# Where a fused attention and MLP kernel loads q, k and v: two quads at the head of each MLP stage, and an output ring of four

## The chip, the cores and the metric

The kernel runs on one core of a Trainium2 chip. The metric is the device time of one launch in microseconds (us); lower is better.

## The reference

Forgetting attention (causal attention whose scores get the sum of log forget gates between key and query), followed by an MLP with the tanh form of GELU:

```python
def _attn_ref(q, k, v, f):                    # each [8, 8, 576, 64]; f is [8, 8, 576]
    scores = scale * np.matmul(q, k.transpose(0, 1, 3, 2))
    cum = np.cumsum(np.log(np.clip(f, 0.0001, 1.0)), axis=-1)
    decay = cum[:, :, :, None] - cum[:, :, None, :]
    scores = np.where(causal, -1000000000.0, scores + decay)
    attn = softmax(scores)                    # written out with max, exp and sum
    return np.matmul(attn, v)

def _moe_ref(x, w_in, w_out):                 # x [4608, 512], w_in [512, 2048], w_out [2048, 512]
    h = x @ w_in
    return gelu_tanh(h) @ w_out

x = attn_out.transpose(0, 2, 1, 3).reshape(4608, 512)
out = _moe_ref(x, w_in, w_out)                # [4608, 512] float32
```

## The kernel before, in words

**Work.** The 64 heads (8 batches of 8) are taken in 16 *quads* of four heads; quad i belongs to batch i // 2. The 4608 rows of the MLP are taken in nine *chunks* of 512, numbered 0 to 8. q and k of a quad are loaded by GpSimd's DMA queue (`load_one`, line 192), which turns them from float32 to bfloat16 on the way, into `q_c` and `k_c`; v of a batch is loaded in five pieces of 128 rows (`load_v`, line 169) into `v_nat`, mostly on SP's queue. All three have two buffers: quad i uses buffer i % 2, batch b buffer b % 2. VectorE transposes q and k (line 198); the scores are matmuls (line 261), their exponentials ScalarE's (line 269), the causal mask is cut by GpSimd (line 275) or multiplied in by VectorE (line 304), `vw` is v times a weight (line 215), and two kinds of products with the exponentials (line 329) give denominators and attention output, which VectorE writes into `xT` (line 360). The first MLP product (lines 374, 422 and 464) goes through GELU on ScalarE into `gT`; the second (line 510; line 580 for chunk 0) goes through VectorE's additions (line 535) into a buffer of the ring `ostage` and is stored by SP (line 523).

**Order.** Everything is issued in an order written out by hand, each engine working through its own instructions in that order. `SETUP` and `FRONT` hold the start: quads 0 to 6 and the chunks 0 and 1. `TABLES[c]` holds chunk c, for c from 2 to 8. A word is an operation with its arguments:

- `LK.i`, `LQ.i`: load k or q of quad i (GpSimd's queue). `TK.i`, `TQ.i`: transpose it (VectorE). A load waits until the transpose that last read its buffer is done.
- `LV` (in a table, chunk c): load v of batch c + 2 (SP). `LV.b.h`: half h (four heads) of batch b on SP. `LX.b.h`: the same on GpSimd's queue. `@` names a load that must be done first.
- `S.i.r`, `M.i.r`, `m.i.r`: scores, mask on GpSimd, mask on VectorE, of round r. `D.i`: denominators. `V.i.x`: attention output. `VW.i`, `vw.i`: `vw` on GpSimd or VectorE.
- `I`, `P`, `R`: parts of a chunk's first MLP product. `G`, `U`, `K`, `T`: sums of blocks on VectorE, for a scheme that multiplies 2 by 2 blocks with seven products.
- `F.n`, `f.n`: the next n pieces of the chunk's second product. `O.512`: what is left of the second product of the chunk before.
- `Y`, `X`: the tables for GELU or the exponential are loaded.

In a table, `q3` stands for quad 2c + 3, `q4` for 2c + 4 and so on. What stands up to `X` is called the chunk's **MLP stage** here (O, P, R, G); what comes behind it is its **attention stage**, where scores and products of two quads lie between pieces of the chunk's second product. So chunk 3 loads quad 11 (`q5`) in its MLP stage and quad 12 (`q6`) in its attention stage, chunk 4 quads 13 and 14, chunk 5 quad 15; chunk 2 loads quads 9 and 10 in its MLP stage, behind the transposes of quads 7 and 8, whose loads stand at the end of `FRONT`. `q6` in chunk 5 and beyond names quads that there are not, and nothing is issued.

**What runs ahead.** A load stands in GpSimd's instructions among masks and `vw`; GpSimd gets to it when what stands ahead of it is done, which can be before TensorE has reached that place of the text.

The kernel text, with the lines of the profile:

Of the kernel before, what the change touches and what calls it, by code (L numbers as in the profile page):

```python
# [8 lines left out]
FP32 = mybir.dt.float32  # L9
# [7 lines left out]
def kernel(  # L17
# [12 lines left out]
    B, H, S, D = q.shape  # L30
    BH = B * H
# [40 lines left out]

    FRONT = """
        TQ.0 B.2.256 TK.1 SB TR LP.2@LQ.0 B.2.128 CW S.0.0 B.5.384 B.1.256 Z TQ.1 vw.0.0 S.0.2 WI.0 LQ.2 M.0.0 B.3.384 H.1.0.1 LP.3 B.1.256 vw.1.0
        WI.1@LU.4 W H.1.1.1 WI.3 B.2.256 WI.2 H.1.0.0 M.1.0.1 D.0.0 M.1.0.0 H.0.1.1 V.0.0.0 H.0.1.0 B.2.256 M.0.1 H.1.1.0 V.0.1.0 D.1.0 H.0.3.0 B.2.128
        V.1.0.0 LX.1.1 H.0.3.1 V.1.1.0 m.0.3.2 H.1.3.0 m.0.3.4 B.1.256 VW.1.1 H.1.3.1 B.4.128 vw.0.1 D.0.1 M.1.3 S.1.2 M.1.1 LK.2 V.0.1.1 V.0.0.1 WO.0
        J.0.1 D.1.1 J.0.0 WO.1@LV.1.1 V.1.1.1 V.1.0.1 J.0.3 WO.2@WI.1 VW.3 J.1.0 WO.3 LK.3 LQ.3 J.1.1 TQ.2 J.1.3 LQ.4 LX.1.0@WO.2 TK.2 J.0.2 J.1.2 X
        LK.4 F.0.6 TK.3 B.3.256 S.2.0 LK.5 F.0.9 S.2.2 F.0.10 S.2.1 TQ.3 TQ.4 F.0.10 LV.2.0@LK.5 m.2.1 vw.2 TK.4 S.3.0 f.0.1 M.2.2 CL.2 LQ.5 M.2.0 D.2
        f.0.6 S.3.1 m.3.0 F.0.6 V.2.0 S.3.2 TK.5 LK.6 M.3.2 f.0.7 V.2.1 CL.3 S.4.1 m.3.1 LQ.6 F.0.6 TQ.5 H.4.2.1 D.3 H.4.0.1 LQ.7 VW.4 H.4.0.0 V.3.1
        v.3.0 f.0.3 H.4.2.0 CL.4 I.1.0 m.4.1 U.0 LV.2.1@LQ.5 I.1.4 TQ.6 m.4.2.3 I.1.1 I.1.5 U.1 LV.3.0@LQ.7 m.4.2.2 TK.6 G.0 M.4.0 I.1.2 I.1.3 U.3  # L80
        I.1.6 I.1.7 G.1.1.2 U.2 X F.1.16 S.5.0 f.1.26 S.5.1 D.4 M.5.0 f.1.16 S.5.2 V.4.0 m.5.2.3 f.1.10 VW.5 V.4.1 CL.5 m.5.2.2 LQ.8 S.6.0 f.1.10 M.5.1
        D.5 f.1.7 S.6.1 V.5.1 f.1.12 V.5.0 vw.6 S.6.2 m.6.1 M.6.2.2 m.6.0 m.6.2.3 LK.7 LK.8 CL.6 LX.3.1@LK.6
    """

    HOMES = {1: 0, 3: 1}
# [5 lines left out]
    """  # L91
    TABLES[3] = """
        Y O.512 P.0.1 R.1 P.4.1 R.1 R.1 TK.q3 TQ.q3 LK.q5 LQ.q5 M.q2.2 LV P.2 G.0 P.3 P.6 P.7 G.1.1.2 X F.10 S.q3.0 D.q2 M.q3.0 f.22 S.q3.1 V.q2.0
        K.3.3 TK.q4 TQ.q4 M.q3.1 VW.q3 f.18 S.q3.2 V.q2.1 M.q3.2 TK.q5 LK.q6 LQ.q6 CL.q3 f.16 S.q4.0 VW.q4 D.q3 M.q4.0 f.18 S.q4.1 TQ.q5 V.q3.0 M.q4.1
        f.13 V.q3.1 T f.3 CL.q4 S.q4.2
    """
    TABLES[4] = """
        Y O.512 P.0.1 R.1 P.4.1 R.1 R.1 LK.q5 LQ.q5 M.q2.2 LV R.3 P.2.1 R.3 G.0.1.2 P.6 R.3 G.0.3.4 G.1.1.2 X F.10 S.q3.0 D.q2 M.q3.0 f.22 S.q3.1
        V.q2.0 TK.q4 TQ.q4 M.q3.1 VW.q3 f.18 S.q3.2 V.q2.1 M.q3.2 TK.q5 LK.q6 LQ.q6 CL.q3 f.16 S.q4.0 VW.q4 D.q3 M.q4.0 f.18 S.q4.1 TQ.q5 V.q3.0 M.q4.1
        f.13 V.q3.1 T f.3 CL.q4 S.q4.2  # L100
    """
    TABLES[5] = """
        Y O.512 P.0.1 R.1 P.4.1 R.1 R.1 LK.q5 LQ.q5 M.q2.2 LV R.3 P.2.1 R.3 G.0.1.2 P.6 R.3 G.0.3.4 G.1.1.2 X F.10 S.q3.0 D.q2 M.q3.0 f.22 S.q3.1
        V.q2.0 TK.q4 TQ.q4 M.q3.1 VW.q3 f.18 S.q3.2 V.q2.1 M.q3.2 TK.q5 LK.q6 LQ.q6 CL.q3 f.16 S.q4.0 VW.q4 D.q3 M.q4.0 f.18 S.q4.1 TQ.q5 V.q3.0 M.q4.1
        f.13 V.q3.1 T f.3 CL.q4 S.q4.2
    """
    TABLES[6] = """
        Y O.512 P.0.1 R.1 P.4.1 R.1 R.1 LK.q5 LQ.q5 M.q2.2 LV R.3 P.2.1 R.3 G.0.1.2 P.6 R.3 G.0.3.4 G.1.1.2 X F.10 S.q3.0 D.q2 M.q3.0 f.22 S.q3.1
# [7 lines left out]
    """  # L116

    singles = ctx.enter_context(tc.tile_pool(name="singles", bufs=1))
    ostage_pool = ctx.enter_context(tc.tile_pool(name="ostage", bufs=3))
    snap_pool = ctx.enter_context(tc.tile_pool(name="snap", bufs=4))  # L120
    den_pool = ctx.enter_context(tc.tile_pool(name="den", bufs=1))
    rb_pool = ctx.enter_context(tc.tile_pool(name="rb", bufs=2))
# [4 lines left out]
    def many(n, shape, dtype, name):  # L127
        return [singles.tile(shape, dtype, name=f"{name}{i}") for i in range(n)]
# [11 lines left out]
    vw = many(2, [128, NT + 1, 4, D], BF16, "vw")  # L140
# [4 lines left out]
    g1, g2, g4 = many(3, [128, HF, HC], BF16, "gsum")  # L145
    u1, u2, u4 = many(3, [128, HF, HD], BF16, "usum")
    w_in_sb = singles.tile([128, N_DT, D_FF], BF16, name="w_in_sb")
    w_out_sb = singles.tile([128, N_FT, D_MODEL], BF16, name="w_out_sb")
    f_sb = singles.tile([BH, S], FP32, name="f_sb")
    logfT = singles.tile([128, NT * BH], FP32, name="logfT")  # L150
    before = singles.tile([128, (NT - 1) * BH], FP32, name="before")
    wT = singles.tile([128, NQ, NT, 4], FP32, name="wT")
# [635 lines left out]
```

## Time and profile before

| | us |
|---|---|
| median of 3 runs | 331.43 |
| lowest and highest of them | 329.97, 331.58 |
| the profiled execution, its own time | 330.9 |
| its span, from the first to the last instruction | 329.2 |
| TensorE busy (matmuls) | 314.4 |
| VectorE, ScalarE, GpSimd busy | 241.3, 203.0, 111.6 |
| mean granted TensorE clock | 0.999 of full speed |

| stage (start to end in the span, us) | MLP | attention |
|---|---|---|
| chunk 2 | 102.57 to 116.39 | 116.39 to 138.30 |
| chunk 3 | 138.30 to 151.72 | 151.72 to 174.36 |
| chunk 4 | 174.36 to 187.53 | 187.53 to 208.94 |
| chunk 5 | 208.94 to 222.12 | 222.12 to 242.62 |

A stage starts here with its first matmul of the first or of the second product on TensorE. "Busy" of TensorE holds matmuls whose ends are modelled. In the profile's lists, a row of waits names an engine's instruction and what ended its idle time; "issue" is idle time that ended with nothing the profile shows. Of the DMA queues, q0 carries GpSimd's loads, q1 SP's loads and stores, and q8 the packets of kind "instruction". A share of the DMA engines is the time that packets took, over the time of 16 engines; it can come out over 100% where packets overlap.

### The profile page before, as it was taken

To read this page: it belongs to the slowest core of one execution; us is meant where nothing else is said; L and a number is where in the kernel's file an instruction comes from. 1 tells how busy PE (TensorE), PEld (TensorE's weight loads), DVE (VectorE), ACT (ScalarE), POOL (GpSimd) and SP (SyncE) were. 2 spreads that over 40 slices of the span, in tenths; PEclk is the share of its full clock that TensorE was granted. 3 is DMA by queue.
4 is the path that set the end of the run, shared out by engine and by line. 5 is a ranking of instruction groups with operands and counts; after the bars stand their busy time and mean duration, and the time that the engine had idled before them with its cause. 6 is when DMAs were issued, how large, how long until landed. Compare 5 with 4: busy or idle time off the path is not lost.

```text
span 329.2 us, 12196 instructions
## 1 busy us (share of the span) xinstructions
PE 314.4 (96%) x5479; PEld 214.8 (65%) x5499; DVE 241.3 (73%) x381; ACT 203.0 (62%) x245; POOL 111.6 (34%) x155
## 2 busy tenths in 40 slices
PE   3999999999999999999979999999999999999995
PEld 1357844544766467766766677667776787687684
DVE  4676139894867866878967899679977957785772
ACT  4685677775767576577647785668666951721630
POOL 8986563510414418202761038201820150000000
PEclk9999999999999999999999999999999999999999
DMA  7999999771124990184178415941020002012003
GB/s 119 210 215 214 171 230 206 149 167 31 36 40 94 234 208 31 66 177 75 36 149 172 68 37 106 193 92 36 8 95 0 26 14 98 0 35 96 3 32 98
DMA packets 44325, 33.45 MB, mean 102 GB/s; under 512 B 27488, under 2 KB 37856, under 8 KB 44272
## 3 DMA queue, kind: packets, MB, share of 16 engines
q0 software_dynamic: 8848, 16.58, 28.7%
q1 hardware_dynamic: 35280, 16.01, 18.6%
q8 instruction: 43, 0.70, 0.9%
q14 instruction: 10, 0.08, 0.1%
q10 hardware_dynamic: 144, 0.07, 0.1%
HBM read 36.85 MB, written 9.44 MB: 141 GB/s over the span
## 4 chain that ended last, share of the span: by engine, by line
PE 93%; POOL 2%; issue 2%; DVE 1%; DMA 1%; ACT 0%; POOLq 0%; DVEq 0%; ACTq 0%
PE ps_w L510 29%; PE ps_h L374 22%; PE ps_s L261 10%; PE po L329 10%; PE ps_cd L422 6%; PE ps_ab L422 5%; PE ps_h L464 4%; PE pso L580 4%; PE po_m L315 1%; PE idle_ps L240 1%; POOL v_nat L169 1%; DMA out_dram<-o_st 1%; PE ps_o L329 0%; DVE pt L304 0%; PE cum_ps L640 0%
## 5 line engine op out<-in xcount | busy, mean ns | idle before, releaser
L269 ACT ACTIVATE pt<-ps_s 128x1024 bf16<-128x1024 f32 (+2 forms) x100 | 93.7, 988 | 40.9 <-PE ps_s L261 36.4
L275 POOL TENSOR_SCALAR_AFFINE_SELECT pt<-pt 128x512 bf16<-128x512 bf16 (+3 forms) x65 | 39.2, 612 | 126.1 <-ACT pt L269 125.1
L374 PE MATMUL ps_h<-xT,w_in_sb 128*128 128x512 bf16 x320 | 75.7, 379 | 0.8
L381 ACT ACTIVATE gT<-ps_h 128x1024 bf16<-128x1024 f32 x42 | 42.9, 1022 | 41.1 <-PE ps_h L374 40.6
L374 PEld LDWEIGHTS <-w_in_sb 128*128 128x128 bf16 x336 | 32.8, 98 | 34.6 <-issue 0.4
L510 PEld LDWEIGHTS <-gT 128*32 128x32 bf16 (+1 forms) x1247 | 51.0, 97 | 6.7 <-issue 2.7
L510 PE MATMUL ps_w<-w_out_sb,gT 128*32 128x256 bf16 (+1 forms) x1050 | 47.2, 273 | 0.0
L510 PEld LDWEIGHTS <-gsum 128*32 128x32 bf16 (+1 forms) x1256 | 39.4, 97 | 1.4
L261 PE MATMUL ps_s<-qT,kT 32*128 32x64 bf16 (+5 forms) x896 | 36.7, 264 | 0.5 <-issue 0.4
L198 DVE STREAM_TRANSPOSE kT<-k_c 128x576 f32<-128x576 f32 x16 | 19.9, 1247 | 17.5 <-DMA k_c<-in_k_dram 17.5
L510 PE MATMUL ps_w<-usum,gsum 128*32 128x256 bf16 (+1 forms) x832 | 30.7, 273 | 0.0
L215 POOL TENSOR_TENSOR vw<-v_nat,wT 128x1280 bf16<-128x1280 f32 (+1 forms) x13 | 30.4, 2337 | 0.1
L535 DVE TENSOR_TENSOR o_st<-ps_w,snap 128x512 f32<-128x512 f32 x31 | 21.3, 690 | 10.7 <-PE ps_w L510 9.3
L261 PEld LDWEIGHTS <-kT 32*128 32x128 bf16 x896 | 16.7, 93 | 17.7 <-issue 12.9
L360 DVE TENSOR_TENSOR xT<-po,rb 128x576 bf16<-128x576 f32 x26 | 19.5, 752 | 9.5 <-PE po L329 9.0
L329 PE MATMUL po<-pt,vw 128*32 128x64 bf16 (+4 forms) x624 | 23.2, 278 | 1.7 <-issue 1.7
L329 PEld LDWEIGHTS <-vw 128*32 128x32 bf16 x672 | 14.5, 96 | 12.5 <-issue 6.0
L198 DVE STREAM_TRANSPOSE qT<-q_c 128x576 f32<-128x576 f32 x16 | 19.9, 1245 | 1.3 <-PE ps_s L261 0.7
L422 PEld LDWEIGHTS <-w_in_sb 128*128 128x128 bf16 x176 | 17.2, 98 | 5.1 <-issue 0.8
L431 ACT ACTIVATE gT<-snap 128x512 bf16<-128x512 f32 x33 | 18.9, 623 | 0.7
L510 PE MATMUL ps_w<-usum,gT 128*128 128x256 bf16 (+1 forms) x197 | 17.2, 273 | 0.7 <-issue 0.7
L169 POOL DMA_DIRECT2D v_nat<-in_v_dram x20 | 15.3, 776 | 4.7 <-DMA w_out_sb<-in_moe_w_out_dram 4.7
(100 smaller groups left out, 419.4 us busy)
## 6 DMA issues: line engine op xcount, KB each, us to landing
out_dram<-o_st SPq DMA_DIRECT2D x35, 256.0 KB, 2.6
k_c<-in_k_dram POOLq DMA_DIRECT2D x16, 288.0 KB, 5.4
q_c<-in_q_dram POOLq DMA_DIRECT2D x16, 288.0 KB, 6.0
v_nat<-in_v_dram SPq DMA_DIRECT2D x16, 256.0 KB, 5.1
w_in_sb<-in_moe_w_in_dram POOLq DMA_DIRECT2D x4, 512.0 KB, 10.1
w_out_sb<-in_moe_w_out_dram POOLq DMA_DIRECT2D x4, 512.0 KB, 8.4
v_nat<-in_v_dram SPq DMA_DIRECT2D x16, 128.0 KB, 3.3
v_nat<-in_v_dram POOLq DMA_DIRECT2D x13, 128.0 KB, 7.0
```

The lines of the kernel that those rows point to most:

```text
L198: nc.vector.transpose(out=dst.rearrange("p s c -> p (s c)").bitcast(FP32) .rearrange("p (t a) -> p a t", a=S // 32), in_=src.rearrange("p ...
L215: eng.tensor_mul(vw[i % 2][:, t0:t1], vb[:, t0:t1, h0:h0 + 4, :], wT[:, i, t0:t1, :].unsqueeze(3).to_broadcast([128, t1 - t0, 4, D]))
L261: nc.tensor.matmul(tiles[h // 2][:, h % 2, c0:c0 + nq], key_columns(i, key, h, c), qq[32 * h:32 * h + 32, q0:q0 + nq, c], start=(c == 0 an ...
L269: nc.scalar.activation(p[:, 2 * g:2 * g + 2, off:off + n], t[:, :, 0:n], AF.Exp, scale=scale)
L275: nc.gpsimd.affine_select(out=x, in_=x, compare_op=ALU.is_ge, fill=0.0, base=0, pattern=pattern, channel_multiplier=-1)
L329: nc.tensor.matmul(po[r0:r0 + w.shape[-1], 448 + q0:448 + q0 + nq], w, p[:, h, col:col + nq], start=(key in (0, "low")), stop=(key in ("lo ...
L360: nc.vector.tensor_mul(xT[:, 2 * u + x, S * b + s0:S * b + s1], po, rbs[i, part])
L374: nc.tensor.matmul(ph[:, j, :], w_in_sb[:, dt, 128 * ft:128 * ft + 128], xT[:, dt, CH * c:CH * (c + 1)], start=(dt == 0), stop=(dt == N_DT ...
L381: nc.scalar.activation(gT[:, 2 * pr:2 * pr + 2, :], ph, AF.Gelu_apprx_tanh)
L422: nc.tensor.matmul(ps[:, j], w[:, dt, 128 * j:128 * j + 128], x[:, dt], start=(first and j == 0 and dt == 0), stop=(dt == 1), skip_group_c ...
L510: nc.tensor.matmul(ps[c0:c0 + width, n, cols[0]:cols[1]], x[:, j, 128 * n + c0:128 * n + c0 + width], w[:, j, cols[0]:cols[1]], start=(fir ...
L535: nc.vector.tensor_add(st, ps, kept[name])
```

## The change

- `LK.q6 LQ.q6` leaves the attention stages of chunks 3, 4 and 5 (in chunk 5 it issued nothing). The MLP stages of chunks 4 and 5 get `LK.q4 LQ.q4` at their head, ahead of `LK.q5 LQ.q5`. Quads 12 and 14 are thereby loaded a stage later: together with 13 and 15.
- In `FRONT`, `LK.7 LQ.8 LK.8` move to chunk 1's MLP stage, behind `M.4.0`: `LQ.8` out of chunk 1's attention stage, the other two from the end.
- The second half of batch 3's v moves from the end of `FRONT` (`LX.3.1@LK.6`, on GpSimd's queue) to behind `LV.3.0`, as `LV.3.1` on SP's queue.
- The ring `ostage` has four buffers, not three. The 2 KB a partition that this takes come from `f_sb`, which has no tile of its own any more and lies in `g2`, a tile that is first written in chunk 1.

TensorE's and ScalarE's instructions stay the same, in the same order; so do VectorE's. Five DMA issues go from GpSimd to SP (`LV.3.1`). `TABLES[5]` has the same edit as `TABLES[4]`, and is left out of the diff below.

```diff
     FRONT = """
...
-        v.3.0 f.0.3 H.4.2.0 CL.4 I.1.0 m.4.1 U.0 LV.2.1@LQ.5 I.1.4 TQ.6 m.4.2.3 I.1.1 I.1.5 U.1 LV.3.0@LQ.7 m.4.2.2 TK.6 G.0 M.4.0 I.1.2 I.1.3 U.3
-        I.1.6 I.1.7 G.1.1.2 U.2 X F.1.16 S.5.0 f.1.26 S.5.1 D.4 M.5.0 f.1.16 S.5.2 V.4.0 m.5.2.3 f.1.10 VW.5 V.4.1 CL.5 m.5.2.2 LQ.8 S.6.0 f.1.10 M.5.1
-        D.5 f.1.7 S.6.1 V.5.1 f.1.12 V.5.0 vw.6 S.6.2 m.6.1 M.6.2.2 m.6.0 m.6.2.3 LK.7 LK.8 CL.6 LX.3.1@LK.6
+        LQ.7 VW.4 H.4.0.0 V.3.1 v.3.0 f.0.3 H.4.2.0 CL.4 I.1.0 m.4.1 U.0 LV.2.1@LQ.5 I.1.4 TQ.6 m.4.2.3 I.1.1 I.1.5 U.1 LV.3.0@LQ.7 LV.3.1 m.4.2.2
+        TK.6 G.0 M.4.0 LK.7 LQ.8 LK.8 I.1.2 I.1.3 U.3 I.1.6 I.1.7 G.1.1.2 U.2 X F.1.16 S.5.0 f.1.26 S.5.1 D.4 M.5.0 f.1.16 S.5.2 V.4.0 m.5.2.3
+        f.1.10 VW.5 V.4.1 CL.5 m.5.2.2 S.6.0 f.1.10 M.5.1 D.5 f.1.7 S.6.1 V.5.1 f.1.12 V.5.0 vw.6 S.6.2 m.6.1 M.6.2.2 m.6.0 m.6.2.3 CL.6
     """
...
     TABLES[3] = """
         Y O.512 P.0.1 R.1 P.4.1 R.1 R.1 TK.q3 TQ.q3 LK.q5 LQ.q5 M.q2.2 LV P.2 G.0 P.3 P.6 P.7 G.1.1.2 X F.10 S.q3.0 D.q2 M.q3.0 f.22 S.q3.1 V.q2.0
-        K.3.3 TK.q4 TQ.q4 M.q3.1 VW.q3 f.18 S.q3.2 V.q2.1 M.q3.2 TK.q5 LK.q6 LQ.q6 CL.q3 f.16 S.q4.0 VW.q4 D.q3 M.q4.0 f.18 S.q4.1 TQ.q5 V.q3.0 M.q4.1
-        f.13 V.q3.1 T f.3 CL.q4 S.q4.2
+        K.3.3 TK.q4 TQ.q4 M.q3.1 VW.q3 f.18 S.q3.2 V.q2.1 M.q3.2 TK.q5 CL.q3 f.16 S.q4.0 VW.q4 D.q3 M.q4.0 f.18 S.q4.1 TQ.q5 V.q3.0 M.q4.1 f.13
+        V.q3.1 T f.3 CL.q4 S.q4.2
     """
     TABLES[4] = """
-        Y O.512 P.0.1 R.1 P.4.1 R.1 R.1 LK.q5 LQ.q5 M.q2.2 LV R.3 P.2.1 R.3 G.0.1.2 P.6 R.3 G.0.3.4 G.1.1.2 X F.10 S.q3.0 D.q2 M.q3.0 f.22 S.q3.1
-        V.q2.0 TK.q4 TQ.q4 M.q3.1 VW.q3 f.18 S.q3.2 V.q2.1 M.q3.2 TK.q5 LK.q6 LQ.q6 CL.q3 f.16 S.q4.0 VW.q4 D.q3 M.q4.0 f.18 S.q4.1 TQ.q5 V.q3.0 M.q4.1
-        f.13 V.q3.1 T f.3 CL.q4 S.q4.2
+        Y O.512 LK.q4 LQ.q4 P.0.1 R.1 P.4.1 R.1 R.1 LK.q5 LQ.q5 M.q2.2 LV R.3 P.2.1 R.3 G.0.1.2 P.6 R.3 G.0.3.4 G.1.1.2 X F.10 S.q3.0 D.q2 M.q3.0
+        f.22 S.q3.1 V.q2.0 TK.q4 TQ.q4 M.q3.1 VW.q3 f.18 S.q3.2 V.q2.1 M.q3.2 TK.q5 CL.q3 f.16 S.q4.0 VW.q4 D.q3 M.q4.0 f.18 S.q4.1 TQ.q5 V.q3.0
+        M.q4.1 f.13 V.q3.1 T f.3 CL.q4 S.q4.2
     """
...
-    ostage_pool = ctx.enter_context(tc.tile_pool(name="ostage", bufs=3))
+    ostage_pool = ctx.enter_context(tc.tile_pool(name="ostage", bufs=4))
...
-    f_sb = singles.tile([BH, S], FP32, name="f_sb")
+    f_sb = g2.rearrange("p t n -> p (t n)").bitcast(FP32)[0:BH, 0:S]
```

More of the change, by code (lines that the diff above doesn't have):

```diff
@@ L74 @@
         TQ.0 B.2.256 TK.1 SB TR LP.2@LQ.0 B.2.128 CW S.0.0 B.5.384 B.1.256 Z TQ.1 vw.0.0 S.0.2 WI.0 LQ.2 M.0.0 B.3.384 H.1.0.1 LP.3 B.1.256 vw.1.0
-        WI.1@LU.4 W H.1.1.1 WI.3 B.2.256 WI.2 H.1.0.0 M.1.0.1 D.0.0 M.1.0.0 H.0.1.1 V.0.0.0 H.0.1.0 B.2.256 M.0.1 H.1.1.0 V.0.1.0 D.1.0 H.0.3.0 B.2.128
-        V.1.0.0 LX.1.1 H.0.3.1 V.1.1.0 m.0.3.2 H.1.3.0 m.0.3.4 B.1.256 VW.1.1 H.1.3.1 B.4.128 vw.0.1 D.0.1 M.1.3 S.1.2 M.1.1 LK.2 V.0.1.1 V.0.0.1 WO.0
-        J.0.1 D.1.1 J.0.0 WO.1@LV.1.1 V.1.1.1 V.1.0.1 J.0.3 WO.2@WI.1 VW.3 J.1.0 WO.3 LK.3 LQ.3 J.1.1 TQ.2 J.1.3 LQ.4 LX.1.0@WO.2 TK.2 J.0.2 J.1.2 X
@@ L78 @@
-        LK.4 F.0.6 TK.3 B.3.256 S.2.0 LK.5 F.0.9 S.2.2 F.0.10 S.2.1 TQ.3 TQ.4 F.0.10 LV.2.0@LK.5 m.2.1 vw.2 TK.4 S.3.0 f.0.1 M.2.2 CL.2 LQ.5 M.2.0 D.2
-        f.0.6 S.3.1 m.3.0 F.0.6 V.2.0 S.3.2 TK.5 LK.6 M.3.2 f.0.7 V.2.1 CL.3 S.4.1 m.3.1 LQ.6 F.0.6 TQ.5 H.4.2.1 D.3 H.4.0.1 LQ.7 VW.4 H.4.0.0 V.3.1
-        v.3.0 f.0.3 H.4.2.0 CL.4 I.1.0 m.4.1 U.0 LV.2.1@LQ.5 I.1.4 TQ.6 m.4.2.3 I.1.1 I.1.5 U.1 LV.3.0@LQ.7 m.4.2.2 TK.6 G.0 M.4.0 I.1.2 I.1.3 U.3
-        I.1.6 I.1.7 G.1.1.2 U.2 X F.1.16 S.5.0 f.1.26 S.5.1 D.4 M.5.0 f.1.16 S.5.2 V.4.0 m.5.2.3 f.1.10 VW.5 V.4.1 CL.5 m.5.2.2 LQ.8 S.6.0 f.1.10 M.5.1
@@ L82 @@
-        D.5 f.1.7 S.6.1 V.5.1 f.1.12 V.5.0 vw.6 S.6.2 m.6.1 M.6.2.2 m.6.0 m.6.2.3 LK.7 LK.8 CL.6 LX.3.1@LK.6
+        WI.1@LU.4 W H.1.1.1 WI.3 B.2.256 WI.2 H.1.0.0 M.1.0.1 D.0.0 M.1.0.0 H.0.1.1 V.0.0.0 H.0.1.0 B.2.256 M.0.1 H.1.1.0 V.0.1.0 D.1.0 H.0.3.0
+        B.2.128 V.1.0.0 LX.1.1 H.0.3.1 V.1.1.0 m.0.3.2 H.1.3.0 m.0.3.4 B.1.256 VW.1.1 H.1.3.1 B.4.128 vw.0.1 D.0.1 M.1.3 S.1.2 M.1.1 LK.2 V.0.1.1
+        V.0.0.1 WO.0 J.0.1 D.1.1 J.0.0 WO.1@LV.1.1 V.1.1.1 V.1.0.1 J.0.3 WO.2@WI.1 VW.3 J.1.0 WO.3 LK.3 LQ.3 J.1.1 TQ.2 J.1.3 LQ.4 LX.1.0@WO.2 TK.2
@@ new lines @@
+        J.0.2 J.1.2 X LK.4 F.0.6 TK.3 B.3.256 S.2.0 LK.5 F.0.9 S.2.2 F.0.10 S.2.1 TQ.3 TQ.4 F.0.10 LV.2.0@LK.5 m.2.1 vw.2 TK.4 S.3.0 f.0.1 M.2.2
+        CL.2 LQ.5 M.2.0 D.2 f.0.6 S.3.1 m.3.0 F.0.6 V.2.0 S.3.2 TK.5 LK.6 M.3.2 f.0.7 V.2.1 CL.3 S.4.1 m.3.1 LQ.6 F.0.6 TQ.5 H.4.2.1 D.3 H.4.0.1
+        LQ.7 VW.4 H.4.0.0 V.3.1 v.3.0 f.0.3 H.4.2.0 CL.4 I.1.0 m.4.1 U.0 LV.2.1@LQ.5 I.1.4 TQ.6 m.4.2.3 I.1.1 I.1.5 U.1 LV.3.0@LQ.7 LV.3.1 m.4.2.2
+        TK.6 G.0 M.4.0 LK.7 LQ.8 LK.8 I.1.2 I.1.3 U.3 I.1.6 I.1.7 G.1.1.2 U.2 X F.1.16 S.5.0 f.1.26 S.5.1 D.4 M.5.0 f.1.16 S.5.2 V.4.0 m.5.2.3
@@ L93 @@
         Y O.512 P.0.1 R.1 P.4.1 R.1 R.1 TK.q3 TQ.q3 LK.q5 LQ.q5 M.q2.2 LV P.2 G.0 P.3 P.6 P.7 G.1.1.2 X F.10 S.q3.0 D.q2 M.q3.0 f.22 S.q3.1 V.q2.0
-        K.3.3 TK.q4 TQ.q4 M.q3.1 VW.q3 f.18 S.q3.2 V.q2.1 M.q3.2 TK.q5 LK.q6 LQ.q6 CL.q3 f.16 S.q4.0 VW.q4 D.q3 M.q4.0 f.18 S.q4.1 TQ.q5 V.q3.0 M.q4.1
-        f.13 V.q3.1 T f.3 CL.q4 S.q4.2
+        K.3.3 TK.q4 TQ.q4 M.q3.1 VW.q3 f.18 S.q3.2 V.q2.1 M.q3.2 TK.q5 CL.q3 f.16 S.q4.0 VW.q4 D.q3 M.q4.0 f.18 S.q4.1 TQ.q5 V.q3.0 M.q4.1 f.13
+        V.q3.1 T f.3 CL.q4 S.q4.2
     """
     TABLES[4] = """
-        Y O.512 P.0.1 R.1 P.4.1 R.1 R.1 LK.q5 LQ.q5 M.q2.2 LV R.3 P.2.1 R.3 G.0.1.2 P.6 R.3 G.0.3.4 G.1.1.2 X F.10 S.q3.0 D.q2 M.q3.0 f.22 S.q3.1
-        V.q2.0 TK.q4 TQ.q4 M.q3.1 VW.q3 f.18 S.q3.2 V.q2.1 M.q3.2 TK.q5 LK.q6 LQ.q6 CL.q3 f.16 S.q4.0 VW.q4 D.q3 M.q4.0 f.18 S.q4.1 TQ.q5 V.q3.0 M.q4.1
-        f.13 V.q3.1 T f.3 CL.q4 S.q4.2
+        Y O.512 LK.q4 LQ.q4 P.0.1 R.1 P.4.1 R.1 R.1 LK.q5 LQ.q5 M.q2.2 LV R.3 P.2.1 R.3 G.0.1.2 P.6 R.3 G.0.3.4 G.1.1.2 X F.10 S.q3.0 D.q2 M.q3.0
+        f.22 S.q3.1 V.q2.0 TK.q4 TQ.q4 M.q3.1 VW.q3 f.18 S.q3.2 V.q2.1 M.q3.2 TK.q5 CL.q3 f.16 S.q4.0 VW.q4 D.q3 M.q4.0 f.18 S.q4.1 TQ.q5 V.q3.0
+        M.q4.1 f.13 V.q3.1 T f.3 CL.q4 S.q4.2
     """
     TABLES[5] = """
-        Y O.512 P.0.1 R.1 P.4.1 R.1 R.1 LK.q5 LQ.q5 M.q2.2 LV R.3 P.2.1 R.3 G.0.1.2 P.6 R.3 G.0.3.4 G.1.1.2 X F.10 S.q3.0 D.q2 M.q3.0 f.22 S.q3.1
-        V.q2.0 TK.q4 TQ.q4 M.q3.1 VW.q3 f.18 S.q3.2 V.q2.1 M.q3.2 TK.q5 LK.q6 LQ.q6 CL.q3 f.16 S.q4.0 VW.q4 D.q3 M.q4.0 f.18 S.q4.1 TQ.q5 V.q3.0 M.q4.1
-        f.13 V.q3.1 T f.3 CL.q4 S.q4.2
+        Y O.512 LK.q4 LQ.q4 P.0.1 R.1 P.4.1 R.1 R.1 LK.q5 LQ.q5 M.q2.2 LV R.3 P.2.1 R.3 G.0.1.2 P.6 R.3 G.0.3.4 G.1.1.2 X F.10 S.q3.0 D.q2 M.q3.0
+        f.22 S.q3.1 V.q2.0 TK.q4 TQ.q4 M.q3.1 VW.q3 f.18 S.q3.2 V.q2.1 M.q3.2 TK.q5 CL.q3 f.16 S.q4.0 VW.q4 D.q3 M.q4.0 f.18 S.q4.1 TQ.q5 V.q3.0
+        M.q4.1 f.13 V.q3.1 T f.3 CL.q4 S.q4.2
     """
```

## The prediction

> **What bounds the kernel now.** I read the page first: who is busy, and what the DMA queues carry.
>
> ```profile
> PE 314.4 (96%) x5479; PEld 214.8 (65%) x5499; DVE 241.3 (73%) x381; ACT 203.0 (62%) x245; POOL 111.6 (34%) x155
> q8 instruction: 43, 0.70, 0.9%
> ```
>
> TensorE is the bound, at a granted clock of 0.999, and its first matmul starts at 4.95 us; of the 14.8 us in which it is not busy, only what lies inside its run can be won. The second line is small but will matter: 43 packets of 16,384 B for some 10,980 recorded matmuls and weight loads, so 64 B for each instruction and 256 instructions in a packet. TensorE's program comes in over the same 16 DMA engines as the data.
>
> Next, what TensorE waited for (total, times, longest), the rows after setup:
>
> ```profile
> PE po L329 <- issue: 2.2, 2, 1.7
> ...
> PE ps_w L510 <- issue: 0.7, 1, 0.7
> ...
> PE ps_s L261 <- issue: 0.4, 1, 0.4
> ```
>
> Together 3.4 us, and each ends in "issue": no engine, no semaphore and no data transfer released it. To see where they lie I asked for the attention stages of chunks 3, 4, 5, 2 and 1, each from the first product after the MLP stage to the next MLP stage (columns: stretch, length, busy per engine, clock, share of the DMA engines, GB/s):
>
> ```profile
> 151.72:174.36 22.64, 20.93 (x640) 15.94 (x638) 18.47 (x29) 14.28 (x17) 11.57 (x14) 1.00 0.46 86
> 187.53:208.94 21.41, 20.66 (x640) 15.66 (x638) 19.89 (x32) 15.57 (x19) 11.53 (x15) 1.00 0.35 75
> 222.12:242.62 20.50, 20.50 (x641) 15.71 (x638) 19.41 (x31) 14.67 (x18) 9.22 (x10) 1.00 0.13 42
> 116.39:138.30 21.91, 21.48 (x639) 16.24 (x638) 16.30 (x28) 14.29 (x17) 9.68 (x10) 1.00 0.42 91
> 81.32:102.57 21.25, 20.72 (x612) 16.00 (x611) 15.82 (x24) 14.52 (x17) 5.26 (x5) 1.00 0.22 54
> ```
>
> The first four hold the same 638 weight loads. The one without loads of k and q, chunk 5 (DMA share 0.13), has no gap at all: length and busy time are both 20.50. It is the control. The others are longer by 2.14, 0.91 and 1.41, in the order of their DMA shares. Now the longest gap, in the timeline:
>
> ```profile
> 169.31 0.60 PE L329 MATMUL po<-pt,vw 128*32 128x512 bf16 x11
> ...
> 170.02 0.59 POOL L192 DMA_DIRECT2D k_c<-in_k_dram  x1
> ...
> 171.62 0.48 PE L329 MATMUL po<-pt,vw 128*32 128x448 bf16 x11 [1.71 <-issue]
> ```
>
> The DMA queues just before it, 165.4 to 169.2 (packets, MB, share of 16 engines):
>
> ```profile
> q0 software_dynamic: 270, 0.56, 93.7%
> q1 hardware_dynamic: 92, 0.09, 7.2%
> ```
>
> and from 169.2 to 170.0:
>
> ```profile
> q1 hardware_dynamic: 130, 0.12, 44.3%
> q0 software_dynamic: 14, 0.02, 13.0%
> q8 instruction: 1, 0.02, 7.3%
> ```
>
> The loads LK.12 and LQ.12, issued at 164.06 and 164.65, fill the engines to 101%; the instruction packet gets on when they drain, at 169.28. Undisturbed packets of chunk 5 start 3.7 to 4.0 us apart (224.09, 228.06, 231.82, 235.56, 239.56), so after 163.08 this one was due at 167: some 2.4 late. It took 0.94 and TensorE went on 1.40 after its end. The other three gaps look the same: packets at 93.59, 119.84 and 205.45, gaps that end 1.60, 1.33 and 1.34 after those packets' ends, at 96.09, 122.10 and 207.75. Before each lies a load of q or k: LQ.8 issued at 90.56, LQ.10 at 113.11 (landed 122.4), LQ.14 at 200.38.
>
> Why do the same loads not hurt in an MLP stage? There TensorE takes 88 weight loads and 88 matmuls in 13.17 us, 13 instructions a us; in attention 1,279 in 20.50, 62 a us. A block of 256 lasts about 19 us in the one and 4.1 in the other, against 2.3 for a packet and its entry. Indeed after 169.28 the next packets start at 176.16 and 183.90, beside LK.13, LQ.13 and five V loads, and no gap follows.
>
> **The change, part by part, against the profiled execution (330.9 = span 329.2 and 1.7 around it; the median of the runs is 331.43, 0.5 more).**
>
> *Chunk 3.* LK.12 and LQ.12 leave its attention. Compared weight load by weight load with chunk 4, the stage is already 0.19 longer after its first sixteen loads (1.50 against 1.31: the chunk before it in order, not DMA); the rest of 2.14 is the gap with what follows it: -1.95.
>
> *Chunk 4.* LK.14 and LQ.14 leave: the stage becomes chunk 5's, 21.41 to 20.50: -0.91.
>
> *Chunk 1.* LQ.8 leaves its attention: the gap of 21.25 - 20.72: -0.53.
>
> *Chunk 2.* No load stands in its attention text, but those of its MLP stage run over into it. LK.7 and LK.8 (103.75) and LV.3.1 (104.82) are issued first, VectorE's TK.7 waits for LK.7 until 108.32, and GpSimd issues LK.9 to LQ.10 only behind those transposes, 109.87 to 113.11. With quads 7 and 8 loaded in chunk 1, TK.7 starts when VectorE gets to it, about 105.05, and the four loads go out 3.3 us earlier. Queue q0 then holds four loads. A pair's price: LK.12 and LQ.12 with 165.0 to 170.2 at 74.0% of 5.2, 3.85 us of all engines; two pairs 7.7, and 8.6 beside V (q0 had 89.9% of the engines from 114 to 119.8, both queues full): from 107.6 to 116.2 instead of about 121. V loads on q1 last longer, to about 121. The packet of 119.84 is asked for at about 118, so it no longer meets q0 but still q1. The stage's excess over chunk 5 is 1.41 - 0.19 = 1.22 (its gap, and two short stops behind the next two packets). All or nothing of it can go; I take 0.8, nearer to all, since the packet at 183.90 came through the V loads with no gap: -0.8.
>
> *What is added.* In chunk 1's MLP stage LK.7 goes out behind M.4.0 (GpSimd is free at 67.51), LQ.8 and LK.8 wait for TQ.6 and TK.6 (VectorE ends them at 70.7 and 73.6); GpSimd's next work waits for ScalarE until 86.41, so nobody is queued behind those waits. LV.3.1 leaves GpSimd (five issues of 0.75 at 104.82) and becomes five issues of about 0.58 on SP's queue behind 73.96; SP's next store is at 86.54. The engines idle from 75.5 to 84 now (LV.2.1 and LV.3.0 with a store: 75.0% of 8 us); 5.8 for three loads and 2.7 for half a batch of V (priced below) end the work by about 83, a packet is at 84.35: cost 0, at most one gap like chunk 1's, 0.53. In chunks 4 and 5 four loads stand at the head instead of two. GpSimd reaches them behind M.q4.1 of the chunk before, 170.02 and 205.94 as now; M.q2.2 behind them waits until ScalarE's exponentials anyway. Sum in chunk 4: 7.7, V 6.4 (q1: 86.1% of 176.5 to 184.8, less a store of 0.75) or 5.3 (51.5% of 205 to 219, less two and a half), three stores 2.2: from 171.4 to 187 or 188, while attention starts at 185.4 and its first packet comes at 190.1. In chunk 5: 207.3 to 222 or 223, against 223.2. The MLP stages of chunks 4, 5 and 6 take 13.17, 13.18, 13.17 at DMA shares of 0.68, 0.66, 0.07, so matmuls don't pay for traffic. I take 0; the upper end is a rival below. LK.12's first reader, TK.12, comes after 190.
>
> *Output ring of four and f_sb in g2.* VectorE has no wait for an output store in the profile; beside loads a store lands later (4.6 us at 167.31 against 2.1), yet long before the third store behind it, at 193.62. f_sb is read by 9 us, g2 first written at 77.0. 0.
>
> Sum: 0.53 + 0.8 + 1.95 + 0.91 = 4.2; 330.9 - 4.2 = 326.7. The runs' spread (329.97 to 331.58) I take to be the gaps' own, so I add nothing for the median. Against 331.43 it is -1.4%. About 0.5% (1.66 us) can be told from no change.
>
> **Rivals.**
>
> *Chunk 2's packet stays late.* V loads on q1 hold it as q0 did. Then 3.4 is saved: 327.5. For it: DMA is full there until about 121. Chance 0.12.
>
> *The V tail moves into attention.* If chunks 4 and 5 end their V loads 2 us later than summed, each stage pays what chunk 2 pays now, 1.2: 326.7 + 2.4 = 329.1. Against it: the margins of 0.2 to 3 us above. 0.08.
>
> *Slower: four loads lock out the program.* If a packet must wait until q0 is drained, and q0 shares evenly with q1, four loads take 15.4 us: in chunk 4 the packet starts at 186.8 and enters at 189.1. TensorE, 256 instructions on from 169.91 and without the gap, is dry at 182.5: a gap of 6.6. In chunk 5, 225.0 against 222.7: 2.3. Together 8.9 against 4.2 won: 335.6. It decides once the packet starts after 180.2. For it: the packets at 169.28 and 176.16 came as q0 drained. Against: at 119.84 one came through while q0 (83% of the engines in the next us) was full, and the program's start has more such. 0.06.
>
> *The gaps are not the loads'.* Then they stay: 330.9. For it: the coincidence of load and gap is seen four times, not tested. 0.06. [...]
>
> **How the numbers follow.** Forecast 0.68. The range: 325.7 (all of chunk 2, and half a us of small stops) to 329.4 (takes in the first two rivals); outside are the last two, 0.12. Faster: 0.68 + 0.12 + 0.06 of the tail's 0.08 = 0.86; same: 0.02 + 0.06 = 0.08; slower 0.06.
>
> **What would show it.** Right: TensorE's "issue" rows shrink from 3.4 to under 1; the attention stages of chunks 3 and 4 measure about 20.7 and 20.5, chunk 2's under 21.2; MLP stages stay at 13.2 although their DMA share rises to 0.9 and more. Wrong: a gap in the MLP stage of chunk 4 or 5, with its packet behind q0 (the slower rival); gaps in the first 4 us of those attention stages (the V tail); or chunk 3 still at 22.6 with no load near it.

## The result, and the profile after

| | before | after |
|---|---|---|
| median, us | 331.06 (329.97 to 331.58, 4 runs) | 325.52 (325.05 to 327.2, 4 runs) |
| ratio after to before | | 0.9846, 95% interval 0.9802 to 0.9891 |
| profiled execution: time, span, us | 330.9, 329.2 | 325.69, 324.0 |

The change makes the kernel 1.5% faster. A second timing of the same kernel, against 11 runs of before, gave 325.51 us and 0.985 (0.9818 to 0.9881). Some executions of a kernel are slow, at a mean granted clock of 0.979 to 0.994, and the ratios leave them out: of those below, 3 of 35 of the kernel before (332.70 to 334.01 us), 2 of 12 with the ring alone and 1 of 12 with `FRONT` alone, the one whose profile is shown.

The page's rows for the engines and for TensorE's program:

```profile
PE 312.9 (97%) x5479; PEld 214.5 (66%) x5499; DVE 242.2 (75%) x381; ACT 202.8 (63%) x245; POOL 107.8 (33%) x150
q8 instruction: 43, 0.70, 1.0%
```

TensorE, VectorE and ScalarE work through as many instructions as before, GpSimd through five fewer (the issues that went to SP), in 5.2 us less span. TensorE's waits (total, times, longest) are now all there is behind setup:

```profile
PE pso L580 <- issue: 0.5, 3, 0.2
PE po_m L315 <- DVE pt L304: 0.2, 1, 0.2
```

The rows of `po`, `ps_w` and `ps_s` that ended in "issue" are gone. The attention stages of chunks 3, 4, 5, 2 and 1 (stretch, length, busy per engine, clock, DMA share, GB/s):

```profile
149.81:170.40 20.59, 20.59 (x639) 15.86 (x638) 18.43 (x29) 14.28 (x17) 10.69 (x13) 1.00 0.21 53
183.58:204.09 20.51, 20.51 (x640) 15.73 (x638) 19.41 (x31) 14.67 (x18) 11.35 (x14) 1.00 0.16 44
217.26:237.78 20.52, 20.52 (x641) 15.73 (x639) 19.42 (x31) 14.68 (x18) 9.21 (x10) 1.00 0.14 44
115.73:136.39 20.66, 20.66 (x639) 15.90 (x638) 16.83 (x28) 14.29 (x17) 9.86 (x10) 1.00 0.18 47
81.40:101.92 20.52, 20.52 (x613) 15.94 (x612) 15.81 (x24) 14.52 (x17) 4.66 (x4) 1.00 0.15 47
...
```

In all five, length and TensorE's busy time are the same number. The stages lost 2.05 (chunk 3), 0.90 (chunk 4), 1.25 (chunk 2) and 0.73 us (chunk 1), 4.9 of the 5.2; another 0.3 lies behind the last matmul.

Where these 4.9 us lie can be seen by putting the two traces side by side, weight load by weight load. From chunk 1's attention on, the kernel before falls behind at six weight loads: by 0.72 us at 96.09, 0.62 at 122.10, 0.37 at 126.38, 0.26 at 130.38, 2.05 at 171.62 and 0.91 at 207.75, together 4.93. Apart from the first two us or so behind a stop, the two keep their distance within 0.1 us, with loads and without. So TensorE was not slowed, it was stopped, at single places. Counted from the start of the program, these six come behind 1375, 1759, 1887, 2015, 2911 and 3679 recorded weight loads. Their distances (384, 128, 128, 896, 768) are all multiples of 128, which with as many matmuls is the 256 instructions of one packet.

The MLP stages of chunks 4 and 5, first of the kernel before, then of the changed one, where they carry two pairs and a batch of v:

```profile
174.36:187.53 13.17, 13.06 (x88) 8.60 (x88) 9.90 (x16) 9.24 (x14) 1.22 (x2) 1.00 0.68 136
208.94:222.12 13.18, 13.07 (x89) 8.61 (x89) 9.45 (x14) 8.48 (x13) 1.17 (x2) 1.00 0.66 145
...
170.40:183.58 13.18, 13.08 (x89) 8.61 (x89) 9.93 (x16) 9.25 (x14) 2.01 (x4) 1.00 1.03 199
204.09:217.26 13.17, 13.07 (x88) 8.61 (x88) 9.92 (x16) 9.24 (x14) 1.22 (x2) 1.00 1.02 197
```

Their DMA share went from 0.68 and 0.66 to 1.03 and 1.02, the full 16 engines, and their length stayed: 13.17 and 13.18 before, 13.18 and 13.17 after.

### The profile page after: what moved, and what is told of

The parts are those of the page before. It is cut to its first block, busy times and chain, and to the rows that moved or that the text cites. A ratio compares the mean times of both kernels' runs of the same rounds, so it can differ in the third digit from the quotient of the medians.

```text
span 324.0 us, 12192 instructions
## 1 busy us (share of the span) xinstructions
PE 312.9 (97%) x5479; PEld 214.5 (66%) x5499; DVE 242.2 (75%) x381; ACT 202.8 (63%) x245; POOL 107.8 (33%) x150
## 4 chain that ended last, share of the span: by engine, by line
PE 94%; POOL 2%; issue 1%; ACT 1%; DVE 1%; POOLq 0%; DVEq 0%; ACTq 0%
PE ps_w L510 30%; PE ps_h L374 22%; PE ps_s L261 10%; PE po L329 9%; PE ps_cd L422 6%; PE ps_ab L422 5%; PE ps_h L464 4%; PE pso L580 4%; PE po_m L315 1%; PE idle_ps L240 1%; ACT pt L269 1%; POOL v_nat L169 1%; PE ps_o L329 0%; DVE pt L304 0%; POOL q_c L192 0%
## 5 line engine op out<-in xcount | busy, mean ns | idle before, releaser
L329 PE MATMUL po<-pt,vw 128*32 128x64 bf16 (+4 forms) x624 | 22.5, 279 | 0.0
L489 DVE TENSOR_TENSOR gsum<-gT 128x1024 bf16<-128x1024 bf16 x16 | 11.0, 685 | 11.1 <-ACT gT L381 11.1
```

What stands on the lines that cost most here:

```text
L329: nc.tensor.matmul(po[r0:r0 + w.shape[-1], 448 + q0:448 + q0 + nq], w, p[:, h, col:col + nq], start=(key in (0, "low")), stop=(key in ("lo ...
```

## Experiments

The theory on trial: a load of q or k holds back the next packet of TensorE's program, and TensorE runs dry. The main rival: loads in attention slow TensorE, its operands or GpSimd by themselves. Single executions differ in setup (two of the changed kernel by 1.5 us, below), so stage lengths are compared there, and times only where many runs were made.

### The three parts alone

Each is the kernel before with one part of the diff shown above: e1_tables has the new `TABLES[3]`, `[4]` and `[5]`, e2_front the new `FRONT`, and e3_ring this:

```diff
-    ostage_pool = ctx.enter_context(tc.tile_pool(name="ostage", bufs=3))
+    ostage_pool = ctx.enter_context(tc.tile_pool(name="ostage", bufs=4))
-    f_sb = singles.tile([BH, S], FP32, name="f_sb")
+    f_sb = g2.rearrange("p t n -> p (t n)").bitcast(FP32)[0:BH, 0:S]
```

> The kernel before with the new TABLES[3], [4] and [5] alone: quads 12 and 14 are loaded in the MLP stages of chunks 4 and 5. Theory (the loads hold up the packets of TensorE's program): the attention stages of chunks 3 and 4 fall from 22.64 and 21.41 us to about 20.6 and 20.5, those of chunks 1 and 2 stay at 21.3 and 21.9, and the time falls by 2.9 us against before. Rival (the gain comes from the loads in chunks 1 and 2 or from the ring): no change, 0.

> The kernel before with the new FRONT alone: LK.7, LQ.8, LK.8 and LV.3.1 go out in chunk 1's MLP stage. Theory: the attention stages of chunks 1 and 2 fall from 21.25 and 21.91 us to about 20.5 and 20.7, chunks 3 and 4 keep their gaps of 1.7 and 0.75; the time falls by 2.0 us. If the V loads alone, on SP's queue, also hold up packets, chunk 2 keeps most of its excess and the time falls by 0.7.

> The kernel before with the ring of four output buffers, and f_sb in g2, alone. Theory: nothing waits for an output buffer, so 0, within 0.5 us, and all four gaps stay. Rival (late stores hold VectorE up where loads fill the DMA engines): up to 1 us faster, and the gaps shorter.

Measured over 12 runs each, beside 35 of before (median 330.06, from 327.38 to 334.01): tables 0.9936 (0.9909 to 0.9964), front 0.9941 (0.9907 to 0.9976), ring 1.0003 (0.9974 to 1.0032). In us of 330.06: -2.1 (-1.2 to -3.0) for 2.9 expected, -1.9 (-0.8 to -3.1) for 2.0, and nothing. The product of the three, 0.988, agrees with the whole within its interval.

The tables alone, chunks 1 to 4 in this order:

```profile
81.48:103.27 21.79, 20.73 (x612) 16.03 (x611) 15.81 (x24) 14.52 (x17) 5.26 (x5) 1.00 0.21 53
117.08:138.75 21.67, 21.24 (x639) 16.28 (x638) 16.30 (x28) 14.28 (x17) 9.67 (x10) 1.00 0.42 91
152.17:172.76 20.59, 20.59 (x639) 15.83 (x638) 18.45 (x29) 14.28 (x17) 11.48 (x14) 1.00 0.19 50
185.93:206.44 20.51, 20.51 (x640) 15.71 (x638) 19.41 (x31) 14.68 (x18) 11.35 (x14) 1.00 0.17 48
```

Chunks 3 and 4 are within 0.1 us of the control's length, chunks 1 and 2 keep their gaps; chunk 1's is 1.06 us here and was 0.53, with the same text. `FRONT` alone, chunks 1 to 4 in this order:

```profile
81.55:102.07 20.52, 20.52 (x613) 15.92 (x612) 15.80 (x24) 14.52 (x17) 4.66 (x4) 1.00 0.15 46
115.88:136.54 20.66, 20.66 (x639) 15.89 (x638) 16.82 (x28) 14.29 (x17) 9.85 (x10) 1.00 0.19 50
149.96:174.86 24.90, 22.33 (x639) 16.53 (x638) 18.91 (x30) 15.48 (x18) 11.90 (x15) 0.94 0.47 90
188.25:209.50 21.25, 20.66 (x640) 15.70 (x638) 19.89 (x32) 15.42 (x18) 11.41 (x14) 1.00 0.36 75
```

Here chunks 1 and 2 are clean, chunk 4 keeps a gap (0.59), and chunk 3 is longer than in any other profile: a gap of 2.57, and a clock of 0.94 in its stage (more of that below). With the ring alone all four gaps stayed (0.83, 0.42, 1.98 and 0.74). Each part thus clears the stages it should, and the ring none.

### The same loads, another phase of the program

If packets matter, moving the place where a packet of 256 instructions ends must move the gaps, with every load where it is. Short matmuls on zeros ahead of the first scores do that, 32 of them in e5_shift64 (64 instructions with their weight loads) and 72 in e4_shift144. The edit of the first:

```diff
-        TQ.0 B.2.256 TK.1 SB TR ...
+        TQ.0 B.2.256 B.32.32 TK.1 SB TR ...
```

> As the kernel before with 144 instructions put in, but 64 (32 short matmuls on zeros): packets are asked for 0.95 us earlier in a stage. Theory: in chunk 3 at 13.15 us, just ahead of the pair's 13.6 to 17.5, the next at 16.9: its gap of 1.71 goes. In chunk 4 at 14.35 instead of 15.3: its gap grows from 0.75 to about 1.4. Rival (loads slow TensorE or its operands): 1.7 and 0.75 as before.

With 64, chunks 3 and 4:

```profile
155.06:175.65 20.59, 20.59 (x639) 15.83 (x638) 18.45 (x29) 14.28 (x17) 11.54 (x14) 1.00 0.38 82
188.83:211.52 22.69, 20.72 (x640) 15.79 (x638) 19.43 (x31) 14.67 (x18) 11.46 (x14) 1.00 0.39 81
```

The gap has changed stages: none in chunk 3, with its pair in place (share 0.38), and 1.97 in chunk 4, where 0.75 was. The direction is as expected in both, the size in chunk 4 is over the 1.4 expected. Two changes had not been forecast: chunk 1's gap is gone with LQ.8 still in its attention stage, and chunk 2's grew from 0.42 to 0.77. The rival, for which the phase means nothing, fails. The places tell the same: in this kernel TensorE stops behind 1887 and 3679 recorded weight loads, the second the place where the kernel before stopped in chunk 4. The places stay, the work moves past them.

> The kernel before, every load where it was, with 72 short matmuls on zeros (144 instructions of TensorE, nobody reads them) put in ahead of the first scores, where they cost some 2 to 3 us once. They do nothing but move the places where a packet of 256 instructions ends, by 144 instructions, 2.1 us in attention. Theory: a packet must be asked for within the first 2.1 us of a pair's 3.9 us on the DMA engines to be late enough to matter (late by more than 1.8 us: a block lasts 4.1, a packet and its entry 2.3). In chunk 3 it is asked for at 14.1 us after the stage's start and the pair runs from 13.6 to 17.5; 144 instructions on, packets are asked for at 12.0 and 15.75. In chunk 4, 15.3 becomes 13.2 and 16.95. So the gaps of both chunks go, and the stages measure about 20.7 and 20.5; the time is 330.9 less 2.9 or more, plus the 2 to 3. Rival (loads slow TensorE or its operands themselves): gaps of 1.7 and 0.75 as before, time up by 2 to 3.

With 144, chunks 2, 3 and 4:

```profile
116.36:140.91 24.55, 22.54 (x639) 16.86 (x638) 16.20 (x28) 14.28 (x17) 9.75 (x10) 0.93 0.37 81
154.33:174.92 20.59, 20.59 (x639) 15.84 (x638) 18.45 (x29) 14.27 (x17) 11.54 (x14) 1.00 0.38 82
188.09:208.61 20.52, 20.52 (x640) 15.75 (x638) 19.41 (x31) 14.67 (x18) 11.45 (x14) 1.00 0.33 73
```

Chunks 3 and 4 are free of gaps with all their loads in attention, as expected. What I had not worked out is chunk 2: its packet, at 122.88, fell into the V loads and pairs that run over from the MLP stage, 2.01 us of gap, behind weight load 1887 again. The time, 1.0032 (1.0 to 1.0063), shows no gain; with 2.9 forecast to be won and 2 to 3 to be lost on the added matmuls, none had been expected. These two shifts are no remedy: they move the loss.

### A pair put back, where it meets no packet, and where it does

In `TABLES[5]` of the changed kernel (e11_pair_shift188 has `B.94.32` in `FRONT` besides):

```diff
-        ... M.q3.2 TK.q5 CL.q3 ...
+        ... M.q3.2 TK.q5 LK.q4 LQ.q4 CL.q3 ...
```

> The changed kernel with a pair of loads put back into an attention stage, that of chunk 5, at the place where chunks 3 and 4 of the kernel before had theirs (LK.14 and LQ.14 once more, into buffers that nobody reads again). Same bytes, same queue, same place in the stage as the pairs that went with gaps of 1.71 and 0.75. Theory: in chunk 5 packets are asked for at 13.1 and 16.9 us after the stage's start, the pair runs from 13.6 to 17.5: no gap, at most 0.3. Rival (loads in attention cost by themselves): 0.9 to 2.0 us longer than 20.52.

Chunk 5 with the pair:

```profile
217.30:237.81 20.51, 20.51 (x640) 15.71 (x638) 19.41 (x31) 14.67 (x18) 10.35 (x12) 1.00 0.31 73
```

The DMA share rises from 0.14 to 0.31 and the stage doesn't change. Its packet got on at 230.83, just ahead of the pair (first packet on q0 at 230.85), the next at 234.88, as the pair ended (235.04).

> The changed kernel with the pair put back into chunk 5's attention stage, which cost nothing there, and 94 short matmuls on zeros (188 instructions of TensorE) ahead of the first scores. Theory: in chunk 5 a packet is then asked for at 14.1 us after the stage's start, where chunk 3 of the kernel before had it, inside the pair's 13.6 to 17.5: a gap of 1.7 us there (1 to 2.6), no gap in the other attention stages, which have no loads. Rival (chunk 5 is not sensitive to loads for some other reason): no gap, 20.5.

```profile
218.22:239.31 21.09, 20.89 (x640) 15.85 (x638) 19.42 (x31) 14.68 (x18) 10.33 (x12) 1.00 0.32 73
```

With the phase moved the same pair costs 0.57 us (21.09 against 20.52); the other attention stages stay at their lengths. The sign is right, the size is a third of the 1.7 expected and below the range of 1 to 2.6: the packet started at 233.80, 5.2 after the one before, while the pair still ran (LK.14 landed at 234.46, LQ.14 at 236.63). So in this run a packet was held back beside q0, but it did not wait for the whole pair.

### The other queue

In `TABLES[5]` of the changed kernel, with a new word for a load of batch 6's v:

```diff
-        ... VW.q3 f.18 S.q3.2 ...
+        ... VW.q3 LD f.18 S.q3.2 ...
...
+        "LD": lambda c: load_v(6),
```

> The changed kernel with a whole batch of v loaded once more in chunk 5's attention stage, on SP's queue, behind VW.13 (into a buffer that nobody reads again): about 1.2 MB on queue q1 from some 11.5 us after the stage's start, for 5 us or more. A packet is asked for at about 13.1 us, in the middle of it. If traffic of any queue holds packets until it has drained: late by over 3 us, a gap of 1.5 us or more. If only GpSimd's queue q0 does: no gap, the stage at 20.5.

```profile
217.45:238.79 21.34, 20.78 (x641) 15.90 (x639) 19.43 (x31) 14.68 (x18) 9.20 (x10) 1.00 0.43 99
```

Neither answer: 0.82 us longer, with one gap of 0.56. The packet started at 232.09, 5.25 after the one before it (some 1.5 late by that spacing), when four of the five V loads were still on their way (the last landed at 236.27). In this one execution SP's queue also held a packet back, and did not lock it out.

### Quads 7 and 8 alone, and the change without the ring

In `FRONT` of the kernel before, for e8_k7k8:

```diff
-        ... G.0 M.4.0 I.1.2 I.1.3 U.3
+        ... G.0 M.4.0 LK.7 LK.8 I.1.2 I.1.3 U.3
...
-        ... m.6.2.3 LK.7 LK.8 CL.6 LX.3.1@LK.6
+        ... m.6.2.3 CL.6 LX.3.1@LK.6
```

> The kernel before with LK.7 and LK.8 alone moved into chunk 1's MLP stage; LQ.8 stays in chunk 1's attention stage and the second half of batch 3's v on GpSimd's queue at the end of FRONT. Theory: chunk 1 keeps its gap of about 0.5 (LQ.8), chunk 2's excess over chunk 5 falls from 1.41 us to about 0.2 because its pairs go out 3.3 us earlier; with v's half still ahead of them on q0 (1.1 us) part of it may stay, up to 0.6. Rival (VectorE's wait of 3.3 us for LK.7 costs nothing and chunk 2's loads end too late all the same): 1.2 to 1.4 stays.

Chunks 1 and 2:

```profile
84.65:105.61 20.96, 20.73 (x612) 16.04 (x611) 15.81 (x24) 14.52 (x17) 5.26 (x5) 1.00 0.22 55
119.42:140.44 21.02, 20.86 (x639) 16.09 (x638) 16.46 (x28) 14.28 (x17) 9.77 (x10) 1.00 0.30 69
```

Chunk 1 keeps a gap (0.24), chunk 2's excess over chunk 5 falls to 0.52: most of chunk 2's gain comes from the two early loads, and some 0.4 (21.02 to 20.66) from the rest of `FRONT`. Chunks 3 and 4, whose text is unchanged here, had gaps of 0.69 and 0.94, against 1.71 and 0.75 before.

Then the whole change once more (e9_whole) beside the change without the ring (e10_no_ring: `bufs=3`, and `f_sb` in a tile of its own).

> The changed kernel as it is, timed beside the one without the ring. Theory: no 'issue' gap in any attention stage, about 1.4% below before.

> The changed kernel with the old output ring of three buffers and f_sb in a tile of its own; the loads as in the change. Theory: the same time as the whole change, within 0.3%, and no gap in attention. Rival (with four loads at the head of an MLP stage stores land later, and the fourth buffer saves VectorE a wait): slower than the whole change by up to 1 us, with a wait for an output store in VectorE's rows.

Whole change 325.51 us, 0.985 (0.9818 to 0.9881); without the ring 325.46 us, 0.9855 (0.9821 to 0.9889), 6 runs each. VectorE has no wait for an output store in either. The fourth buffer does nothing here. The profiled execution of the whole change took 326.96 although its attention stages of chunks 1 to 5 were as above (within 0.01 us): it lost 1.5 us at 24.19, where TensorE waited for VectorE's `vw` in setup. That is where the changed kernel's own spread (325.05 to 327.2) was seen to come from, once.

## Why the prediction came out right

**The bound and the mechanism** hold. The rows before said that TensorE stops without a releaser, always behind a load and at a late packet. Two things turned the coincidence into a cause: the parts alone, where the program is the same and the gaps went with the loads, and the shifts, where the loads are the same and the gaps moved. All 20 stops without a releaser of 0.2 us and more that the 13 profiles list from chunk 1's attention to chunk 5's lie, counted from the start of each program, whole multiples of 128 recorded weight loads apart. In the attention stages of the kernel after, TensorE still has some 170 to 260 recorded instructions before such a place when the packet for it starts; in the kernel before, ahead of the four gaps, it had 125, 111, 19 and 79. Why a packet waits beside a load, no run shows.

**The sum** was 4.2 and the stages gave 4.9. Chunk 3: 1.95 forecast, 2.05 measured (the stage stays 0.08 longer than chunk 4's, not 0.19); chunk 4: 0.91 and 0.90. Chunk 1: 0.53 and 0.73. There I had taken the gap of the list of waits, which starts at the modelled end of the last matmul; by the weight loads the same stop cost 0.72. Chunk 2: 0.8 of a possible 1.22, and all of it went (1.25), but not quite as reasoned: the pairs were off q0 at 116.59, near the 116.2 of the sum, while the V loads, which I had on q1 until about 121, ended there at 117.62. The packet came at 117.19, so it met none of the pairs and the last 0.4 us of the V loads; whether V loads alone would have held it was not tried in that stage. These terms and the 0.3 behind the last matmul put the profiled execution, 325.69, 1.0 below the forecast of 326.7. The median, 325.52, lies 1.2 below it, and 0.2 below the range's lower end, which had no room for a better end of the kernel. By the ratio, 331.43 x 0.9846 = 326.3 (324.9 to 327.8).

**Added work at no cost** held: in chunk 1's MLP stage the loads end at 82.8 (forecast: by about 83) ahead of the packet at 84.41; the V loads of chunks 4 and 5 land last at 184.60 and 218.40, one us into the attention stages (183.58 and 217.26), and the packets at 187.76 and 219.29 come behind them. The V tail's margin in chunk 5 is 0.9.

**One step was wrong in its working.** I put chunk 3's packet 2.4 us late, from the spacing of the packets before it. A block lasts 4.1 us (256 instructions at the stage's 62 a us) and a packet with its entry 2.3 (0.94 and 1.40), so by this estimate TensorE can take 1.8 of lateness; a gap of 1.71 then means 3.5, which is also what comes out when 256 instructions are counted back from the stop (to 165.77, with the packet at 169.28). Chunk 4's 0.75 means 2.6. With that, e5 and e6 came out on the right side; e11's 0.57 and chunk 4's 1.97 in e5 did not have the size forecast. The lateness itself varies by 1 us and more from one execution to the next: in four kernels with the same text in the stage and the same phase, chunk 3's gap was 1.71, 1.98, 2.57 and 0.69, chunk 1's 0.53, 0.83, 1.06 and 0.24. That chunk 3's forecast of 1.95 came so near is in part luck: it was read from one execution.

**The rivals.** The packet that stays late in chunk 2 and the V tail did not come. "The gaps are not the loads'" is refuted by the parts alone: each takes away the gaps of the stages whose loads it moves. "Loads slow TensorE itself" is refuted by the shifts, and by the weight loads that keep their distance outside the six places. How far TensorE got without its next packet was small: 64 instructions ahead of everything moved a gap from one stage to another (1.71 us in chunk 3 before, 1.97 in chunk 4 with them), and in the attention stages of the kernel after the packets started when TensorE had some 170 to 260 instructions left. The slower rival, a lock-out by four loads, did not come, but it was not put to the test either: in chunk 4 the packet of 168.36 got on ahead of the four loads (on q0 from 170.05 to 178.71) and the next came at 180.09; in chunk 5 they came at 202.92 and 219.29, around 203.69 to 212.77. No packet started beside four loads, by margins of 0.8 us at the least. What four loads would do to a packet was not tried.

## What to carry to other kernels

Where one engine is the bound and its idle time ends in "issue", look at the queue of kind "instruction": here the program came over the same 16 DMA engines as the data, in 43 packets of 16,384 B. By the estimate above, a stage with many short instructions (62 a us) had some 2 us of slack (4.1 for a block, less 2.3) where a stage with long ones (13 a us) had some 17 (19 less 2.3). Put bulk loads where the busiest engine issues slowly; here a full DMA cost nothing there (13.17 us at a share of 0.07 and of 1.02). Judge such a placement by several runs: with the loads in attention the same kernel took from 327.4 to 331.9 us in 32 of 35 runs, and a packet's lateness differed by 1 us and more from one execution to the next.

## What the runs showed that I had not expected

**A gap of 2.01 us cost twice.** In e4 TensorE's gap in chunk 2:

```profile
125.44 0.98 PE L510 MATMUL ps_w<-usum,gsum 128*32 128x256 bf16 x18 [2.01 <-issue]
```

and two stretches of the same kernel behind it (the granted clock is the third number from the end):

```profile
125.80:129.10 3.30, 3.30 (x67) 2.36 (x55) 0.00 (x0) 0.58 (x1) 1.69 (x1) 0.50 0.02 5
129.20:140.90 11.70, 11.70 (x368) 9.00 (x365) 9.36 (x17) 6.97 (x8) 5.44 (x6) 1.00 0.09 27
```

The clock is at 0.50 for 3.4 us, and TensorE takes 20 matmuls a us in it instead of 31; the stage's 24.55 is the clean 20.6, the gap's 2.0 and 1.9 more. `FRONT` alone shows it after its gap of 2.57: 0.50 from 171.89 to 175.30, where that stage's 24.90 is the clean 20.6, the gap and 1.7 more. Gaps of 1.98 (ring alone) and 1.97 (64 instructions) kept the clock at 1.00.

The length of a gap or wait alone did not decide it: in e5 and e8 the clock was at half for 13.65 and 10.24 us of setup, behind waits of only 0.63 and 0.59, and chunk 1's MLP stage ended 4.3 and 3.3 us later than before. In the 13 traces every stretch between two changes of the granted clock is a whole number of 3.41 us (314.03 and 310.61 us at 1.00 in the kernels before and after, 92 and 91 of them), as if it were set in steps. Counted by these steps, the two gaps that were followed by a halved clock left 2.01 and 2.25 us idle in one step, while those of 1.98 and 1.97 were cut by the border of a step, into 1.54 and 0.44 in the one and 0.44 and 1.53 in the other. No run tested whether the idle time in a step decides it, and the waits of 0.63 and 0.59 speak against its being all. In the kernel before, a mean clock of 0.995 or less, as one such step of 3.41 us gives it, is seen in 3 of the 35 runs, with `FRONT` alone in 3 of 12, with 144 instructions in 8 of 12, with the tables alone in none of 12.

**A packet's way.** A packet of 16,384 B took 0.88 to 1.9 us on its engine in all 13 profiles, beside loads and without. The waiting (3.5 us by the estimate above, ahead of the gap of 1.71) came before it, not in it.
